# Transposing the last stage's tiles on VectorE and through DRAM instead of on TensorE

## The chip, the cores and the metric

One core of a Trainium2 chip runs the whole program. The metric is the device time of one execution in microseconds (us); lower is better. Engines are named as the profile names them: PE is TensorE (PEld its weight loads), DVE is VectorE, ACT is ScalarE, POOL is GpSimd, SP is SyncE, whose queue issues the DMA transfers spoken of here.

## The reference

Three steps follow each other: causal attention with a compressive memory over 4 batches of 8 heads (576 positions, 64 wide), then two feed-forward blocks over the 2304 tokens. The change is in the second of these and in the weights it loads:

```python
def _moe2_ref(x, w_in, w_out, g_ln):          # x 2304x512, w_in 512x1024, w_out 1024x512
    h = x @ w_in
    e = np.exp(h - np.max(h, axis=-1, keepdims=True))
    solu = h * (e / (np.sum(e, axis=-1, keepdims=True) + 1e-09))
    mu = np.mean(solu, axis=-1, keepdims=True)
    var = np.mean((solu - mu) ** 2, axis=-1, keepdims=True)
    ln = (solu - mu) / np.sqrt(var + 1e-06) * g_ln
    return (ln @ w_out).astype(np.float32)
```

## The kernel before

The kernel has three stages: attention (class `Attention`), the first feed-forward block (class `Moe1`), the second (class `Moe2`). Only the last one and the loading of its weights are touched. Each engine runs its instructions in the order in which the program issues them; waits between engines are semaphores that a framework derives from the reads and writes of tiles. A tile's tag with `bufs=n` means that n buffers are used in turn, so a new tile of the tag waits for the readers of the one n before it.

Every matrix product here is made of three: operands are split into a high part (rounded to the fp32r format) and a low part (the rest), and high x high, high x low and low x high are summed in PSUM.

The last stage works on 18 tiles (`NTL`) of 128 tokens. For tile i:

- `y_split` (helper `split_y`): ScalarE copies the high part of the tile's input (128x512), GpSimd subtracts for the low part.
- `h_mm` (L829): the first products, 24 matrix products of 512 columns into a PSUM tile H of 128x1024 (tag S, two buffers).
- `top` (L840): VectorE takes the row maximum.
- `norm`: ScalarE's exponent with its row sum (L849); on VectorE sum and reciprocal (L850, L851), the product of H and softmax (L852), mean and variance (L854, L855, L856); on GpSimd the power -0.5 of the variance (L857); on VectorE again the scaling (L858), from SBUF to SBUF in place. The result is `e`, with tokens in the partitions.
- `t_step`: the second product needs the other layout, features in the partitions. TensorE transposes eight 128x128 blocks into two PSUM tiles (tag T, two buffers, L868); ScalarE copies the high part to `L` (L875), VectorE subtracts for the low part (L876), both straight from PSUM.
- `o_mm` (L898): the second products, 24 of 512 columns into a PSUM tile O (tag X, one buffer); ScalarE copies the result to `ob` (L905), SP's queue writes it out (L906).

The loop issues for i: inputs of i+2, first products of i+1, their maximum, transposes of i, normalisation of i+1, second products of i-1. The first products of tile 0 and its normalisation are issued ahead of the loop, beside the last slice of the first block. In the last iteration tile 16's second products are split in two halves around tile 17's transposes. At i = 0 the loader finishes the last weights.

The weights come as 64-bit values through `Weights`: `_fetch` issues a load of raw words on SP's queue, `_convert` turns them to fp32 on ScalarE, VectorE and GpSimd and splits them; rows of `w_out` are scaled by `g_ln` (tile `gl`), and at most one further load is fetched ahead of the conversion that runs. The tiles of w_out are `w2o`, `w2o_a`, `w2o_b` and `w2o_c` with two blocks of 128 rows each; the last block is finished during the last stage's start. The last two of them and the inputs of the first two tiles lie in buffers that the first block has left.

Of the kernel before, what the change touches and what calls it, by code (L numbers as in the profile page):

```python
# [9 lines left out]
F32 = mybir.dt.float32  # L10
F32R = mybir.dt.float32r
U32 = mybir.dt.uint32
AF = mybir.ActivationFunctionType
ALU = mybir.AluOpType
AX = mybir.AxisListType
P = 128

DRAIN = 3

# [662 lines left out]
class Weights:  # L682
# [3 lines left out]
    N = 512  # L686
# [14 lines left out]

    def _fetch(self):
        hi, lo, src, scale = self.todo.pop(0)
        words = src.shape[-1] // hi.shape[-1]
        raw = self.pool.tile([P, words * self.N], U32, tag="raw", name="raw", bufs=2)
        rv = raw
        if len(hi.shape) == 3:
            rv = raw.rearrange("p (c f) -> p c f", f=src.shape[-1])
        self.nc.sync.dma_start(out=rv, in_=src)
        self.raw.append((hi, lo, raw, words, scale))  # L710

    def fetch(self):
# [82 lines left out]
class Moe2:  # L795
# [43 lines left out]
        mx = s[:, 0:1]  # L839
        self.nc.vector.tensor_reduce(mx, self.st[i]["H"], AX.X, ALU.max, negate=True)  # L840

    def norm(self, i, e=None):
        nc, FF, tp = self.nc, self.FF, self.tp
        H, s = self.st[i]["H"], self.st[i]["s"]
        mx, z, mv = s[:, 0:1], s[:, 1:2], s[:, 2:4]
        bs = s[:, 4:].rearrange("p (a b) -> p a b", b=6)
        if e is None:
            e = tp.tile([P, FF], F32, tag="e", name=f"e2_{i}")
        nc.scalar.activation(e, H, AF.Exp, bias=mx, accum_out=z)  # L849
        nc.vector.tensor_scalar_add(z, z, 1e-9)  # L850
        nc.vector.reciprocal(z, z)  # L851
        nc.vector.scalar_tensor_tensor(e, H, z, e, ALU.mult, ALU.mult)  # L852
        for a in range(FF // 512):
            nc.vector.bn_stats(bs[:, a, :], e[:, a * 512 : (a + 1) * 512])  # L854
        nc.vector.bn_aggr(mv, bs)  # L855
        nc.vector.tensor_scalar_add(mv[:, 1:2], mv[:, 1:2], 1e-6)  # L856
        nc.gpsimd.tensor_tensor(mv[:, 1:2], mv[:, 1:2], self.half, ALU.pow)  # L857
        nc.vector.tensor_scalar(e, e, mv[:, 0:1], mv[:, 1:2], ALU.subtract, ALU.mult)  # L858
        self.st[i]["e"] = e

    def t_step(self, i):
        nc, KF = self.nc, self.KF
        e = self.st[i]["e"]
        L = self.tp.tile([P, 2, KF, P], F32R, tag="L", name=f"L{i}")
        for a in range(KF // 4):
            T = self.ps.tile([P, 512], F32, tag="T", name=f"T2_{i}_{a}", bufs=2)
            for f in range(4):
                nc.tensor.transpose(  # L868
                    T[:, f * P : (f + 1) * P],
                    e[:, (4 * a + f) * P : (4 * a + f + 1) * P],  # L870
                    self.ident,
                )
            Tv = T.rearrange("p (f t) -> p f t", t=P)
            hi = L[:, 0, 4 * a : 4 * a + 4, :]
            nc.scalar.copy(hi, Tv)  # L875
            nc.vector.tensor_tensor(  # L876
                L[:, 1, 4 * a : 4 * a + 4, :], Tv, hi.bitcast(F32), ALU.subtract
            )
        self.st[i]["L"] = L

    def o_mm(self, i, steps, spare=False):
        nc, KF, DM = self.nc, self.KF, self.DM
        L = self.st[i]["L"]
        last = (i + 1) * P == self.out.shape[0]
        if steps[0] == 0:
            tags = "XS" if last else "S" if spare else "X"
            self.st[i]["O"] = [
                self.ps.tile([P, 1024], F32, tag=t, name=f"O{i}{t}", bufs=2 if t == "S" else 1)
                for t in tags
            ]  # L890

        w = DM // 2 if last else DM
        prods = ((0, 0), (0, 1), (1, 0))
        for a in range(0, DM, w):
            O = self.st[i]["O"][a // w][:, 0:w]
            for f in steps:
                for k, (ll, wl) in enumerate(prods):
                    nc.tensor.matmul(  # L898
                        O, L[:, ll, f, :], self.w2o[f][:, wl, a : a + w],
                        start=(f == 0 and k == 0), stop=(f == KF - 1 and k == 2),  # L900
                    )
            if steps[-1] < KF - 1:
                continue
            ob = self.tp.tile([P, w], F32, tag="ob", name=f"ob{i}_{a}")
            nc.scalar.copy(ob, O)  # L905
            nc.sync.dma_start(out=self.out[i * P : (i + 1) * P, a : a + w], in_=ob)  # L906
# [3 lines left out]
def attention_moe_kernel(  # L910
# [3 lines left out]
    nc = tc.nc  # L914
    B, H, S, D = q.shape
    NT, DM = out.shape
    KD = DM // P
    HT = NT // 2
    FF2 = moe2_g_ln.shape[0]
# [6 lines left out]
    xl = ctx.enter_context(tc.tile_pool(name="xl", bufs=2))  # L926
# [4 lines left out]
    tp = ctx.enter_context(tc.tile_pool(name="m1", bufs=2))  # L931
# [3 lines left out]
    gl = cpool.tile([P, FF2 // P], F32, tag="gl", name="gl")  # L935
# [19 lines left out]
    with ExitStack() as ea, ExitStack() as es:  # L955
        att = Attention(
            ea.enter_context(tc.tile_pool(name="att", bufs=2)),
            es.enter_context(tc.tile_pool(name="scores", bufs=2, side="right")),
            ps, tc, q, k, v, M_prev, z_prev, beta, xT, ident,
        )  # L960
        att.loader = loader
        for s in range(2):
            m.load_slice(s)

        def start_moe1():

            xh1 = eb.enter_context(tc.tile_pool(name="xh1", bufs=nblk - 2, side="right"))
            xh.append(xh1)
            for n in (2, 3):
                drain.add(split_x(n, xh1))  # L970

        rooms = att.between = Between()
        drain = Between()

        def filler():
            rooms.finish()
            for n in range(2):
                H = ps.tile([P, m.KF, 512], F32, tag="S", name=f"H0_{n}", bufs=2)
                yield from m.h_step(0, n, H, per=4)

        fill = filler()
        some = islice(fill, 11)
        todo = [
            (rooms, lambda p: att.done == 4, lambda: split_x(0, xh0)),
            (rooms, lambda p: att.done == 8, lambda: split_x(1, xh0)),
        ]
        with tc.manual_schedule():
            for p, i in att.run(some):
                if att.scores == 0:
                    es.close()  # L990
                    start_moe1()
                    att.scores = -1
                if (p, i) == (att.NP // 2, 0):
                    nc.sync.dma_start(out=gl, in_=moe2_g_ln.rearrange("(c p) -> p c", p=P))
                if todo and todo[0][1](p):
                    where, _, steps = todo.pop(0)
                    where.add(steps())
                if att.scores < 0 and i % DRAIN == 0:
                    drain()
            for _ in fill:  # L1000
                pass
            drain.finish()
# [5 lines left out]
    KF2 = FF2 // P  # L1008
# [3 lines left out]
    def add_w2(t, c, src, r, scale):  # L1012

        nf = t.shape[3]
        N = loader.N
        k = src.shape[1] // nf
        for a in range(0, nf, N):
            loader.add(
                t[:, 0, c, a : a + N],
                t[:, 1, c, a : a + N],  # L1020
                src[r * P : (r + 1) * P, a * k : (a + N) * k],
                gl[:, r : r + 1] if scale else None,
            )

# [30 lines left out]
    m2 = Moe2(tc, w2i, w2o, y0, yT, out, cpool, ps, ident)  # L1055
    with eb:
        eb.enter_context(tc.manual_schedule())
        items = [(s, n) for s in range(m.NS) for n in range(nblk)]
        for i, (s, n) in enumerate(items):
# [19 lines left out]
            else:  # L1079
                loader.pump()  # L1080
        m2.tp = tp
        m2.y_split(0)
        m2.h_mm(0)
        m2.top(0)
        G = tp.tile([P, 2 * m.KF * NB], F32, tag="G", name="e2_0", bufs=2)
        m2.norm(0, G[:, 0:FF2])
        m.y_step(*items[-1], ps, yT)
    m2.tp = ctx.enter_context(tc.tile_pool(name="m2", bufs=2))
    ctx.enter_context(tc.manual_schedule())
    NTL = NT // P  # L1090
    half = KF2 // 2
    m2.y_split(1)
    for i in range(NTL):
        if i + 2 < NTL:
            m2.y_split(i + 2)
        if i + 1 < NTL:
            m2.h_mm(i + 1)
            m2.top(i + 1)
        else:
            m2.o_mm(i - 1, range(half), True)  # L1100
        if i == 1:
            m2.norm(2)
            m2.o_mm(0, range(KF2))
        m2.t_step(i)
        if i + 1 < NTL:
            if i != 1:
                m2.norm(i + 1)
            if i > 1:
                m2.o_mm(i - 1, range(KF2))
        else:  # L1110
            m2.o_mm(i - 1, range(half, KF2))
            m2.o_mm(i, range(KF2))
        if i == 0:
            while loader.raw or loader.todo:
                loader.pump()
            loader.finish()


def split_y(nc, Y, src):
# [32 lines left out]
```

## Time and profile before

| | |
|---|---|
| device time, median of 3 runs | 829.36 us (829.1 to 829.38) |
| span of the profiled execution, first to last instruction | 826.7 us |
| PE busy | 801.9 us, 97% of the span, 4936 products |
| DVE busy | 577.8 us, 70% |
| ACT busy | 348.8 us, 42% |
| POOL busy | 344.3 us, 42% |
| mean granted TensorE clock | 0.994 of full speed |

The profile shows one execution, and its span; a device time of that one execution is not recorded apart from the runs, whose median is 2.7 us above the span. The last stage runs from about 605.9 us to the end. Busy times are sums over stages with different limits, so what a change in one stage is worth has to be read from that stage's rows.

### The profile page before, as it was taken

The page shows a single profiled execution, that of the slowest core. Times are in us where ns is not written, and L with a number is a line of the kernel's source. Part 1 is how long each engine was busy: PE and PEld are TensorE (multiplying, and loading weights), DVE is VectorE, ACT ScalarE, POOL GpSimd, SP SyncE. Part 2 cuts the span into 40 slices and gives each one's busy share as a digit, 9 for nine tenths or more (in the row PEclk, how much of TensorE's full clock was granted, in tenths as well). Part 3 has the DMA queues.
Part 4 walks back from the last instruction along what each step waited for, and adds up shares of the span by engine and source line. Part 5 has one row for each costly group of instructions (what it writes and reads, how often), then busy time and mean ns, then how long its engine had stood idle before and what let it go on. Part 6 is the DMA issues. An engine that isn't in the chain of part 4 may idle for free.

```text
span 826.7 us, 13172 instructions
## 1 busy us (share of the span) xinstructions
PE 801.9 (97%) x4936; PEld 705.4 (85%) x4936; DVE 577.8 (70%) x1130; ACT 348.8 (42%) x726; POOL 344.3 (42%) x380
## 2 busy tenths in 40 slices
PE   2799999999999999999999999999999999999998
PEld 1566666676899999999999999999998888888887
DVE  3999999994367777777775675766878555455553
ACT  1788898886333323232323232322423222222222
POOL 4888899998623333233432130322532111111110
PEclk9899999999999999999999999999999999999999
DMA  7567778671111212121211020201100000000001
GB/s 172 134 153 186 164 146 172 151 168 35 55 51 53 75 52 77 52 77 52 77 52 52 26 76 2 72 31 40 63 1 13 26 13 25 27 26 14 25 26 39
DMA packets 64655, 56.84 MB, mean 69 GB/s; under 512 B 48848, under 2 KB 49104, under 8 KB 64592
## 3 DMA queue, kind: packets, MB, share of 16 engines
q1 hardware_dynamic: 64208, 54.86, 24.8%
q10 hardware_dynamic: 384, 1.15, 0.5%
q8 instruction: 39, 0.64, 0.3%
q14 instruction: 24, 0.20, 0.1%
HBM read 46.55 MB, written 4.72 MB: 62 GB/s over the span
## 4 chain that ended last, share of the span: by engine, by line
PE 92%; DVE 3%; DMA 2%; POOL 1%; issue 1%; ACT 1%; ACTq 0%; DVEq 0%; POOLq 0%
PE H L608 24%; PE Y L637 24%; PE H L829 12%; PE T L377 5%; PE X L401 5%; PE S L267 4%; PE T L868 2%; PE S_L L281 2%; PE R L218 2%; PE X L359 1%; DMA k<-in_k_dram 1%; DVE sc L291 1%; PE O16S L898 1%; PE O10X L898 1%; PE O14X L898 1%
## 5 line engine op out<-in xcount | busy, mean ns | idle before, releaser
L637 PE MATMUL Y<-G,wo 128*128 128x384 f32 x1152 | 207.9, 335 | 0.2 <-DVE yT L649 0.2
L637 PEld LDWEIGHTS Y<-G,wo 128*128 128x128 f32 x1152 | 200.7, 188 | 0.5 <-ACT xh L575 0.4
L608 PE MATMUL H<-xh,wi 128*128 128x384 f32 x768 | 158.2, 338 | 0.0
L783 POOL TENSOR_TENSOR cvw<-cvw,cva 128x512 f32<-128x512 f32 x48 | 62.7, 1306 | 198.3 <-DVE cva L781 122.3
L608 PEld LDWEIGHTS H<-xh,wi 128*128 128x128 f32 x768 | 136.0, 189 | 1.4 <-issue 1.4
L621 ACT ACTIVATE t<-H 128x768 f32<-128x768 f32 x48 | 39.1, 814 | 216.3 <-PE H L608 216.3
L622 DVE TENSOR_TENSOR t<-H,t 128x768 f32<-128x768 f32 x48 | 45.9, 957 | 63.5 <-ACT t L621 63.5
L829 PE MATMUL H<-w2i,Ys 128*128 128x512 f32 x384 | 90.0, 390 | 0.0
L608 PE MATMUL H<-xT,wi 128*128 128x384 f32 x384 | 90.0, 338 | 0.0
L337 POOL TENSOR_SCALAR P<-P,sm,og 128x128 f32<-128x128 f32 (+3 forms) x128 | 86.7, 687 | 6.1 <-DVE sm L328 2.6
L829 PEld LDWEIGHTS H<-w2i,Ys 128*128 128x128 f32 x384 | 72.0, 188 | 15.0
L651 DVE TENSOR_TENSOR yT<-Y,yT 128x384 f32<-128x384 f32 (+1 forms) x126 | 79.0, 682 | 0.0
L624 DVE TENSOR_TENSOR G<-t,G 128x768 fp32r<-128x768 f32 x48 | 46.5, 968 | 43.3 <-ACT G L623 43.3
L857 POOL TENSOR_TENSOR s<-s,nhalf 128x1 f32<-128x1 f32 x18 | 9.9, 553 | 153.3 <-DVE s L856 143.9
L313 ACT ACTIVATE P<-sc,mx 128x128 f32<-128x128 f32 (+3 forms) x128 | 70.8, 558 | 5.7 <-DVE mx L291 5.6
L608 PEld LDWEIGHTS H<-xT,wi 128*128 128x128 f32 x384 | 68.6, 188 | 0.2 <-issue 0.2
L384 ACT COPY pt<-T 128x512 f32<-128x512 f32 (+1 forms) x95 | 54.3, 608 | 26.5 <-PE T L377 26.2
L267 PE MATMUL S<-kT,qT 64*128 64x512 f32 (+3 forms) x256 | 46.3, 486 | 19.5 <-DVE kT L182 18.6
L840 DVE TENSOR_REDUCE s<-H 128x1 f32<-128x1024 f32 x18 | 22.0, 1224 | 60.2 <-PE H L829 60.2
L623 ACT CAST G<-t 128x768 fp32r<-128x768 f32 x48 | 40.1, 835 | 51.2 <-DVE t L622 51.2
L291 DVE CUSTOM_DVE_ANT_0 sc<-S,mask 128x128 f32<-128x128 f32 (+3 forms) x128 | 55.7, 483 | 5.3 <-PE S L267 4.8
L875 ACT CAST L<-T 128x512 fp32r<-128x512 f32 x36 | 19.4, 590 | 80.4 <-PE T L868 80.4
(267 smaller groups left out, 1264.5 us busy)
## 6 DMA issues: line engine op xcount, KB each, us to landing
raw<-in_moe_w_in_dram SPq DMA_DIRECT2D x24, 512.0 KB, 3.7
raw<-in_moe_w_out_dram SPq DMA_DIRECT2D x24, 512.0 KB, 3.4
q<-in_q_dram SPq DMA_DIRECT2D x64, 140.0 KB, 3.1
out_dram<-ob SPq DMA_DIRECT2D x17, 256.0 KB, 2.0
v<-in_v_dram SPq DMA_DIRECT2D x32, 128.0 KB, 3.4
xT<-x SPq DMA_DIRECT2D x16, 256.0 KB, 3.0
k<-in_k_dram SPq DMA_DIRECT2D x24, 140.0 KB, 3.6
k<-in_k_dram SPq DMA_DIRECT2D x32, 72.0 KB, 3.3
```

Of the source, the lines that this page charges most:

```text
L267: nc.tensor.matmul(s, Q[rows, P * r : P * r + P], K[rows, 0:w], start=True, stop=True, skip_group_check=True,)
L291: self.nc.vector.tensor_tensor_reduce(out=sc, in0=s, in1=mask, scale=-0.125, scalar=3.0e38, op0=ALU.add, op1=ALU.min, accum_out=self.mx[p] ...
L313: self.nc.scalar.activation(t, self.sc.pop((p, i)), AF.Exp, bias=self.mx[p][:, i : i + 1], scale=-1.0, accum_out=self.sm[p][:, i : i + 1],)
L337: self.nc.gpsimd.tensor_scalar(d, d, self.sm[p][:, i : i + 1], og, ALU.mult, ALU.mult)
L384: self.copy(pt, T)
L608: nc.tensor.matmul(H[a:z, f], wi[:, wl, c, f * P + a : f * P + z], self.x[n][xl][:, c], start=(count[f] == 0), stop=(count[f] == 3 * KD - ...
L622: nc.vector.tensor_tensor(t, H, t, ALU.subtract)
L624: nc.vector.tensor_tensor(G[:, 1], t, G[:, 0].bitcast(F32), ALU.subtract)
L637: nc.tensor.matmul(Y[d][:, 0:NB], wo[:, wl, f, d * P : (d + 1) * P], G[:, gl, f], start=(i == 0), stop=(i == 3 * KF - 1),)
L651: nc.vector.tensor_tensor(y, src, y, ALU.add)
L783: self.eng.tensor_tensor(w, w, a, ALU.add)
L829: nc.tensor.matmul(H[:, nh * 512 : (nh + 1) * 512], Y[:, yl, c, :], w2i[:, wl, c, nh * 512 : (nh + 1) * 512], start=(k == 0), stop=(k == 3 ...
```

## The change

For tiles 1 to 15 `t_step` is replaced. `norm` is split into `exp` and the rest. `turn` transposes the normalised tile on VectorE, which does so within each square of 32x32 and leaves the square in its place; the result (tile `rest`, two buffers) is written to DRAM, 512 KB, and read back by four transfers, one for each quarter of 32 partitions, which bring the squares to the quarter where they belong. `spread` then makes the high part on ScalarE and the low part on GpSimd, from SBUF, with the columns put in order by the access pattern. The order of features that results is another than before: partition quarter i holds features 256 i to 256 i + 255. So the rows of w_out and of `g_ln` are loaded in that order, in four pieces each, and tiles 0, 16 and 17, which are still transposed on TensorE (`direct`), are scaled to a permuted place.

The loop issues for i from 1: inputs of i+1, first products of i, maximum and exponent of i, the high part of i-1, the rest of the normalisation of i, the low part of i-1, VectorE's transpose and the transfers of i, second products of i-2. The second products of a tile thus stand two iterations after its first ones, and within them all products with the high part come first. Tiles 16 and 17 are transposed and multiplied after the loop.

```diff
@@ _fetch
-        self.nc.sync.dma_start(out=rv, in_=src)
+        n = P // len(parts)
+        for i, part in enumerate(parts):
+            self.nc.sync.dma_start(out=rv[i * n : (i + 1) * n], in_=part)
@@ Moe2
+    def exp(self, i, e=None):
         H, s = self.st[i]["H"], self.st[i]["s"]
-        mx, z, mv = s[:, 0:1], s[:, 1:2], s[:, 2:4]
+        if e is None:
+            e = self.tp.tile([P, self.FF], F32, tag="e", name=f"e2_{i}")
+        self.nc.scalar.activation(e, H, AF.Exp, bias=s[:, 0:1], accum_out=s[:, 1:2])
+        self.st[i]["e"] = e
+
+    def norm(self, i, direct=False):
...
-        nc.vector.tensor_scalar(e, e, mv[:, 0:1], mv[:, 1:2], ALU.subtract, ALU.mult)
-        self.st[i]["e"] = e
+        to = e
+        if direct:
+
+            t = self.st[i]["e"] = self.rest[:, i % 2]
+            to = t.rearrange("t (c i p) -> t i c p", i=4, p=Q)
+            e = e.rearrange("t (i c p) -> t i c p", i=4, p=Q)
+        nc.vector.tensor_scalar(to, e, mv[:, 0:1], mv[:, 1:2], ALU.subtract, ALU.mult)
+
+    def turn(self, i):
+
+        nc, FF = self.nc, self.FF
+        e, T, R = self.st[i]["e"], self.rest[:, i % 2], self.rest[:, 2 + i % 2]
+        nc.vector.transpose(T, e)
+        D = self.dram.tile([P, FF], F32, tag="D", name=f"D{i}", bufs=3)
+        nc.sync.dma_start(out=D, in_=T)
+        src = D.rearrange("(j p) (i n) -> i p j n", p=Q, i=4)
+        for q in range(4):
+            nc.sync.dma_start(
+                out=R[q * Q : (q + 1) * Q].rearrange("p (j n) -> p j n", j=4), in_=src[q]
+            )
+        self.st[i]["R"] = R
+
+    def spread(self, i):
+        nc, KF = self.nc, self.KF
+        L = self.st[i]["L"] = self.tp.tile([P, 2, KF, P], F32R, tag="L", name=f"L{i}")
+        R = self.st[i]["R"].rearrange("p (j c t) -> p c j t", j=4, t=Q)
+        hi, lo = (L[:, k].rearrange("p c (j t) -> p c j t", t=Q) for k in range(2))
+        nc.scalar.copy(hi, R)
+        yield
+        nc.gpsimd.tensor_tensor(lo, R, hi.bitcast(F32), ALU.subtract)
@@ o_mm
-        prods = ((0, 0), (0, 1), (1, 0))
+        order = [(f, 0, wl) for f in range(KF) for wl in range(2)] + [(f, 1, 0) for f in range(KF)]
+        half = len(order) // 2
+        steps = range(half * part[0], half * (part[-1] + 1))
@@ attention_moe_kernel
-                    nc.sync.dma_start(out=gl, in_=moe2_g_ln.rearrange("(c p) -> p c", p=P))
+                    rows = moe2_g_ln.rearrange("(i c p) -> i p c", i=4, p=Q)
+                    for j in range(4):
+                        nc.sync.dma_start(out=gl[j * Q : (j + 1) * Q], in_=rows[j])
...
+    direct = (0, NTL - 2, NTL - 1)
     m2.y_split(1)
-    for i in range(NTL):
-        if i + 2 < NTL:
-            m2.y_split(i + 2)
+    for i in range(1, NTL):
         if i + 1 < NTL:
-            m2.h_mm(i + 1)
-            m2.top(i + 1)
-        else:
-            m2.o_mm(i - 1, range(half), True)
+            m2.y_split(i + 1)
+        m2.h_mm(i)
+        m2.top(i)
+        m2.exp(i)
+        lo = iter(())
         if i == 1:
-            m2.norm(2)
-            m2.o_mm(0, range(KF2))
-        m2.t_step(i)
-        if i + 1 < NTL:
-            if i != 1:
-                m2.norm(i + 1)
-            if i > 1:
-                m2.o_mm(i - 1, range(KF2))
-        else:
-            m2.o_mm(i - 1, range(half, KF2))
-            m2.o_mm(i, range(KF2))
-        if i == 0:
+            m2.t_step(0)
+        elif i - 1 not in direct:
+            lo = m2.spread(i - 1)
+            next(lo)
+        m2.norm(i, i in direct)
+        next(lo, None)
+        if i not in direct:
+            m2.turn(i)
+        if i > 1:
+            m2.o_mm(i - 2)
+        if i == 1:
             while loader.raw or loader.todo:
                 loader.pump()
             loader.finish()
+    m2.t_step(NTL - 2)
+    m2.o_mm(NTL - 2, (0,))
+    m2.t_step(NTL - 1)
+    m2.o_mm(NTL - 2, (1,))
+    m2.o_mm(NTL - 1)
```

## Rows read from the trace of the kernel before

**Rows 1.** Busy time: window, length, us and instructions per engine, clock, DMA.
```profile
660.00:680.00 20.00, 20.00 (x97) 16.68 (x96) 11.14 (x19) 5.47 (x10) 2.02 (x3) 1.00 0.04 14
```

**Rows 2.** Chain of waits, one tile of the last stage: start us, us, what.
```profile
674.92 0.87 PE T L868 x8
675.79 5.53 PE O4X L898 x24
681.32 5.45 PE H L829 x24
```

**Rows 3.** Chain of waits, start of the last stage.
```profile
621.22 0.88 PE T L868 x8
622.09 5.48 PE H L829 x24
627.57 5.53 PE O0X L898 x24
```

**Rows 4.** Chain of waits, end of the last stage.
```profile
805.91 5.47 PE O15X L898 x24
811.38 2.77 PE O16S L898 x12
815.02 2.77 PE O16S L898 x12
```

**Rows 5.** Groups by line, 665 to 827 us: busy us, mean ns, idle before.
```profile
L876 DVE TENSOR_TENSOR L<-T,L 128x512 fp32r<-128x512 f32 x27 | 17.3, 682 | 2.6 <-ACT L L875 2.6
L875 ACT CAST L<-T 128x512 fp32r<-128x512 f32 x26 | 14.0, 590 | 60.6 <-PE T L868 60.6
```

**Rows 6.** Line L182, VectorE's transposes: ns min/median/max, first and last start us.
```profile
L182 DVE STREAM_TRANSPOSE kT<-k x16: 758/1003/1260, 9.4 to 181.7; 128x576 f32<-128x576 f32 x16
```

**Rows 7.** Timeline of VectorE: start us, us, what, idle before and its releaser.
```profile
621.25 1.23 DVE L840 TENSOR_REDUCE s<-H 128x1 f32<-128x1024 f32 x1 [0.40 <-PE H L829]
623.90 0.15 DVE L850 TENSOR_SCALAR s<-s 128x1 f32<-128x1 f32 x1 [0.23 <-ACT e L849]
628.01 1.77 DVE L858 TENSOR_SCALAR e<-e,s 128x1024 f32<-128x1024 f32 x1 [0.68 <-POOL s L857]
629.70 1.21 DVE L840 TENSOR_REDUCE s<-H 128x1 f32<-128x1024 f32 x1
636.27 1.77 DVE L858 TENSOR_SCALAR e<-e,s 128x1024 f32<-128x1024 f32 x1 [0.67 <-POOL s L857]
...
811.93 0.81 DVE L858 TENSOR_SCALAR e<-e,s 128x1024 f32<-128x1024 f32 x1 [0.73 <-POOL s L857]
```

**Rows 8.** Timeline of GpSimd.
```profile
627.94 1.29 POOL L792 TENSOR_TENSOR w2o_c<-cvw,w2o_c 128x512 fp32r<-128x512 f32 x1
```

**Rows 9.** Timeline of ScalarE.
```profile
622.65 1.13 ACT L849 ACTIVATE e<-H,s 128x1024 f32<-128x1024 f32 x1
633.13 0.59 ACT L905 COPY ob<-O0X 128x512 f32<-128x512 f32 x1 [0.98 <-PE O0X L898]
```

**Rows 10.** DMA issues by line: count, KB each, median us to landing.
```profile
raw<-in_moe_w_out_dram SPq DMA_DIRECT2D x24, 512.0 KB, 3.4
out_dram<-ob SPq DMA_DIRECT2D x17, 256.0 KB, 2.0
v<-in_v_dram SPq DMA_DIRECT2D x32, 128.0 KB, 3.4
```

**Rows 11.** Line L709, weight loads on SP's queue: ns of an issue, min/median/max.
```profile
L709 SPq DMA_DIRECT2D raw<-in_moe_w_out_dram x24: 327/340/550, 63.3 to 594.1; - x24
```

**Rows 12.** TensorE near the kernel's start: timeline, then busy time by stretch.
```profile
23.14 3.89 PE L267 MATMUL S<-kT,qT 64*128 64x512 f32 x16 [6.38 <-DVE kT L182]
33.26 1.13 PE L267 MATMUL S<-kT,qT 64*128 64x512 f32 x4 [1.47 <-DVE kT L182]
...
25.00:26.00 1.00, 1.00 (x6) 0.68 (x4) 0.63 (x3) 0.00 (x0) 0.82 (x3) 0.50 1.01 255
34.00:35.00 1.00, 1.00 (x6) 0.33 (x6) 1.00 (x3) 0.60 (x4) 0.83 (x2) 1.00 0.82 246
```

More of the change, by code (lines that the diff above doesn't have):

```diff
@@ L16 @@
 P = 128
+Q = 32
 DRAIN = 3
@@ L703, in _fetch @@
         hi, lo, src, scale = self.todo.pop(0)
-        words = src.shape[-1] // hi.shape[-1]
+        parts = src if isinstance(src, list) else [src]
+        words = parts[0].shape[-1] // hi.shape[-1]
         raw = self.pool.tile([P, words * self.N], U32, tag="raw", name="raw", bufs=2)
@@ L707, in _fetch @@
         if len(hi.shape) == 3:
-            rv = raw.rearrange("p (c f) -> p c f", f=src.shape[-1])
-        self.nc.sync.dma_start(out=rv, in_=src)
+            rv = raw.rearrange("p (c f) -> p c f", f=parts[0].shape[-1])
+        n = P // len(parts)
+        for i, part in enumerate(parts):
+            self.nc.sync.dma_start(out=rv[i * n : (i + 1) * n], in_=part)
         self.raw.append((hi, lo, raw, words, scale))
@@ L840, in top @@
         self.nc.vector.tensor_reduce(mx, self.st[i]["H"], AX.X, ALU.max, negate=True)
-    def norm(self, i, e=None):
-        nc, FF, tp = self.nc, self.FF, self.tp
+    def exp(self, i, e=None):
         H, s = self.st[i]["H"], self.st[i]["s"]
-        mx, z, mv = s[:, 0:1], s[:, 1:2], s[:, 2:4]
+        if e is None:
[4 more added lines that the diff above has]
+        nc, FF = self.nc, self.FF
+        H, s, e = (self.st[i][k] for k in ("H", "s", "e"))
+        z, mv = s[:, 1:2], s[:, 2:4]
         bs = s[:, 4:].rearrange("p (a b) -> p a b", b=6)
-        if e is None:
-            e = tp.tile([P, FF], F32, tag="e", name=f"e2_{i}")
-        nc.scalar.activation(e, H, AF.Exp, bias=mx, accum_out=z)
         nc.vector.tensor_scalar_add(z, z, 1e-9)
@@ L857, in norm @@
         nc.gpsimd.tensor_tensor(mv[:, 1:2], mv[:, 1:2], self.half, ALU.pow)
-        nc.vector.tensor_scalar(e, e, mv[:, 0:1], mv[:, 1:2], ALU.subtract, ALU.mult)
-        self.st[i]["e"] = e
+        to = e
[5 more added lines that the diff above has]
+    def turn(self, i):
+        nc, FF = self.nc, self.FF
+        e, T, R = self.st[i]["e"], self.rest[:, i % 2], self.rest[:, 2 + i % 2]
[16 more added lines that the diff above has]
+        nc.gpsimd.tensor_tensor(lo, R, hi.bitcast(F32), ALU.subtract)
     def t_step(self, i):
@@ L867, in t_step @@
             for f in range(4):
[L868 to L872, printed above, removed]
+                nc.tensor.transpose(T[:, f * P : (f + 1) * P], e[:, (4 * a + f) * P : (4 * a + f + 1) * P], self.ident)
             Tv = T.rearrange("p (f t) -> p f t", t=P)
@@ L879, in t_step, with o_mm @@
         self.st[i]["L"] = L
-    def o_mm(self, i, steps, spare=False):
+    def o_mm(self, i, part=(0, 1)):
         nc, KF, DM = self.nc, self.KF, self.DM
@@ L884, in o_mm @@
         last = (i + 1) * P == self.out.shape[0]
-        if steps[0] == 0:
+        spare = part != (0, 1)
+        if 0 in part:
             tags = "XS" if last else "S" if spare else "X"
@@ L892, in o_mm @@
         w = DM // 2 if last else DM
-        prods = ((0, 0), (0, 1), (1, 0))
+        order = [(f, 0, wl) for f in range(KF) for wl in range(2)] + [(f, 1, 0) for f in range(KF)]
+        half = len(order) // 2
+        steps = range(half * part[0], half * (part[-1] + 1))
         for a in range(0, DM, w):
             O = self.st[i]["O"][a // w][:, 0:w]
[L896 to L902, printed above, removed]
+            for k in steps:
+                f, ll, wl = order[k]
+                nc.tensor.matmul(
+                    O, L[:, ll, f, :], self.w2o[f][:, wl, a : a + w],
+                    start=(k == 0), stop=(k == len(order) - 1), skip_group_check=spare,
+                )
+            if 1 not in part:
                 continue
@@ L1017, in add_w2 @@
         for a in range(0, nf, N):
+            cols = slice(a * k, (a + N) * k)
+            if scale:
+                rows = src.rearrange("(i c p) f -> c i p f", i=4, p=Q)[r]
+                part = [rows[i, :, cols] for i in range(4)]
+            else:
+                part = src[r * P : (r + 1) * P, cols]
             loader.add(
@@ L1020, in add_w2 @@
                 t[:, 1, c, a : a + N],
-                src[r * P : (r + 1) * P, a * k : (a + N) * k],
+                part,
                 gl[:, r : r + 1] if scale else None,
@@ L1081, in attention_moe_kernel @@
         m2.tp = tp
+        rest = xl.tile([P, KD * HT], F32, tag="xl", name="rest")
+        m2.rest = rest[:, 0 : 4 * FF2].rearrange("p (n f) -> p n f", f=FF2)
         m2.y_split(0)
@@ L1085, in attention_moe_kernel @@
         G = tp.tile([P, 2 * m.KF * NB], F32, tag="G", name="e2_0", bufs=2)
-        m2.norm(0, G[:, 0:FF2])
+        m2.exp(0, G[:, 0:FF2])
+        m2.norm(0, True)
         m.y_step(*items[-1], ps, yT)
     m2.tp = ctx.enter_context(tc.tile_pool(name="m2", bufs=2))
+    m2.dram = ctx.enter_context(tc.tile_pool(name="dram", bufs=3, space=bass.MemoryType.DRAM))
     ctx.enter_context(tc.manual_schedule())
     NTL = NT // P
-    half = KF2 // 2
+    direct = (0, NTL - 2, NTL - 1)
     m2.y_split(1)
-    for i in range(NTL):
-        if i + 2 < NTL:
-            m2.y_split(i + 2)
+    for i in range(1, NTL):
         if i + 1 < NTL:
-            m2.h_mm(i + 1)
-            m2.top(i + 1)
-        else:
-            m2.o_mm(i - 1, range(half), True)
-        if i == 1:
-            m2.norm(2)
-            m2.o_mm(0, range(KF2))
-        m2.t_step(i)
-        if i + 1 < NTL:
-            if i != 1:
-                m2.norm(i + 1)
-            if i > 1:
-                m2.o_mm(i - 1, range(KF2))
-        else:
-            m2.o_mm(i - 1, range(half, KF2))
-            m2.o_mm(i, range(KF2))
-        if i == 0:
+            m2.y_split(i + 1)
[3 more added lines that the diff above has]
+        lo = iter(())
+        if i == 1:
+            m2.t_step(0)
[9 more added lines that the diff above has]
+        if i == 1:
             while loader.raw or loader.todo:
```

## The prediction

> **What bounds the kernel now.** I read the busy time by stretch first. In the last stage TensorE works every microsecond at the full clock level (granted clock 1.00, 2.4 GHz), while VectorE, ScalarE and GpSimd are busy for 11.1, 5.5 and 2.0 us of the same 20 us [rows 1]. The chain of waits then shows what a tile costs: eight transposes 0.87 us, 24 second products 5.53 us, 24 first products 5.45 us, with no gap between them [rows 2]. So a tile's period is about 11.83 us and TensorE's own work sets it. The chain at the stage's start [rows 3] and end [rows 4] is likewise all TensorE. Something taken off TensorE here shortens the kernel as long as nobody else becomes late; the rest of the argument is a search for who that might be.
>
> **What is removed.** Tiles 1 to 15 lose their TensorE transposes: 15 x 0.87 = 13.1 us [rows 2]. Does a second product run as fast without transposes ahead of it? Tile 16's products stand in two halves of 12, one directly behind tile 15's products, one directly behind transposes, and both take 2.77 us [rows 4]; so I take the whole 13.1 us as gain (lower bound of this term 12.2 us, if each tile gave back the 0.06 us that separates 5.53 from 5.47 [rows 2, 4]). The new order of the products (all with the high part of the tile first, then the low part) leaves their count at 24, and costs nothing by itself. New period: 5.45 + 5.50 = 10.95 us.
>
> **What VectorE pays.** It loses the two subtractions of 0.68 us that read the transposed tile from PSUM [rows 5] and gains one 32x32 transpose of 128x1024. The nearest row is the transposes of 128x576 in the attention stage, 0.758 us where the written side is contiguous, 1.26 us where it isn't [rows 6]. Scaled by 1024/576 that is 1.35 and 2.24 us; here both sides are contiguous, and part of the 0.758 us is fixed, so I take 1.25 us and keep 2.24 us as the upper bound. Per tile, from the start of the maximum to the start of the last scaling, VectorE takes 636.27 - 629.70 = 6.57 us, waits for ScalarE and GpSimd included [rows 7]. With 0.81 us for the scaling (its length in tile 17, where GpSimd has nothing else to do [rows 7]) and 1.25 us for the transpose, tile work ends 8.65 us after the first products: less than 10.95 us, so hidden.
>
> The scaling is not always 0.81 us. In tile 1 and tile 2 it took 1.77 us; in tile 1 GpSimd had just begun a subtraction of two SBUF operands, which ended at 629.23, 0.55 us before the scaling ended at 629.78 [rows 7, 8]. The change moves the low-part subtraction, 128x1024, to GpSimd: two times 1.29 us [rows 8], 2.6 us, queued right behind the small power of the next tile, on which the scaling waits too. If it starts there, the scaling takes 2.6 + 0.55 = 3.15 us and VectorE's work ends after 6.57 + 3.15 + 1.25 = 11.0 us. That is as long as the period; but then the following tile's data are late by 2.3 us, its subtraction starts behind the scaling, and that tile is back at 8.65 us. I cost it at nothing. The Trainium skill ("SBUF — State Buffer", section "Who interferes with whom") has the rule behind this: VectorE in a two-port mode and GpSimd take a shared port pair in turn, whole instructions at a time, while a VectorE instruction with one SBUF input outside those modes is left alone. It would let the scaling be blocked and the new transpose not; it is the fourth rival below.
>
> **What the way through DRAM costs.** One write of 512 KB, which must land, then four reads of 128 KB, each to a quarter of the partitions. No row shows a write that is read back. The write: between the 256 KB output's 2.0 us and the 512 KB weight load's 3.4 us; I take 2.8 us. The reads: 512 KB in one piece lands in 3.4 us; as four issues on SP at 0.33 us each the last starts 1.0 us late, and 128 KB loads of v took 3.4 us, so 3.4 to 4.4 us [rows 10, 11]; I take 4.0 us. With 0.1 us for the two hand-overs: 6.9 us (5.4 to 7.8). The skill's page "SBUF — State Buffer" (section "Door 1: The DMA port swizzle") speaks against the change: a transfer to 32 partitions reaches half of the SBUF ports, at about 218 GB/s at best; four of them in turn would need an estimated 2.4 us beside the fixed part, instead of 1.2 us. The sum by it would be 1.2 us more round trip, so 1.2 us less gain, still in the forecast's own range. No row here shows it.
>
> In the steady state from the end of a tile's first products to the start of its second there are now two periods, 21.9 us. Used are 8.65 + 6.9 + 1.1 (ScalarE's copy of the high part: a pass over 128x1024 took 1.13 us [rows 9]) + 0.6 (the copy of the older tile's output, which stands behind it on ScalarE, and must empty the one PSUM buffer before the next second products start; 0.59 us [rows 9]) = 17.3 us. 4.6 us are left; so a round trip up to 11.5 us is hidden. The low part has 3.7 us more (16 products first). SP's queue holds the output's transfer behind the reads, but the output has two buffers, and nobody waits.
>
> **The start is not the steady state.** Tile 1's first products are followed only by tile 0's transposes (0.87), not by second products, so there is less time. First products of tile 1 end at 621.22 [rows 3]. The maximum ends at 622.48 [rows 7]. The exponent now comes ahead of tile 0's two PSUM copies on ScalarE: 1.13 + 2 x 0.59 us [rows 5, 9], to about 624.8; VectorE's second low part (0.68) ends at 625.45, and only then does the normalisation of tile 1 go on, which it did at 623.90 [rows 7]: 1.55 us later. GpSimd's last weight subtraction moves from 627.94 to 629.5 and ends at 630.8 [rows 8] (the new order wants it at 631.0, the sixteenth of tile 0's products: just hidden; bound 0.5 us). Tile 1's scaling ends 0.55 us behind it, 631.35; transpose 632.6; round trip 639.5; copy 640.6; tile 0's output copy 641.2. TensorE, with tile 1's transposes gone, is there at 627.57 + 5.53 + 5.45 = 638.55 [rows 2, 3]. It waits **2.7 us** (1.2 with the shortest round trip, 3.6 with the longest, 4.6 with the longest transpose too). Behind it wait only third and later tiles, which have their 4 us. Tile 0, 16 and 17 are scaled straight to a permuted layout; if the 0.81 us doubled, at most 0.8 us once.
>
> **The end.** Tile 16 is still transposed on TensorE, but its products follow at once instead of a tile later. Counted from the end of the last first products: tile 15's products to 5.48, transposes to 6.35; ScalarE's output copy 5.5 to 6.1, then the first half of tile 16's copy (0.59) to 6.7. TensorE waits **0.35 us** (0 to 1). Tile 17 is normalised at 6.57 + 0.81 = 7.4, tile 16's low parts are through at 8.75, TensorE wants tile 17 at 6.7 + 2.77 = 9.5: covered.
>
> **Other edits.** The gain vector and the eight scaled weight blocks come in four pieces each: 27 more issues of 0.33 us on SP [rows 11], fetched one conversion ahead; hidden, and up to 1 us once if that cover is gone.
>
> **Sum.** -13.1 + 2.7 + 0.35 = -10.05 us. The profiled span is 826.7 us, so 816.7 us; the median of the runs shown, 829.36 us, lies 2.7 us above the span, for what lies around it, which the change leaves alone: **819.3 us**.
>
> **The rivals.** (1) The forecast, 818 to 820.7 us: 0.55. (2) Tile 1's round trip is hidden as well: 816.4 us. It needs the trip within 4.2 us; the rows' shortest is 5.4. 0.08. (3) The wait at tile 1 lowers the clock. After an idle time of 6.38 us at the kernel's start the granted clock was 0.50, the 1.2 GHz level, still two microseconds after TensorE had gone on; after 1.47 us it was 1.00 [rows 12]. 2.7 us lies between. Some 3 us of work at half speed cost 1.5 us: 820.8 us. 0.20. (4) The lock between scaling and GpSimd's subtraction is met in every tile, and the transpose is as slow as its upper bound or is blocked as well: VectorE needs 6.57 + 3.15 + 2.24 = 12.0 us in tiles that meet it and 9.6 in those that don't. If three tiles of four meet it, the mean is 11.4 us, 14 x 0.45 = 6 us lost: 825 us. 0.10. (5) Slower: the round trip sets the pace. Each tile's second products wait for its data, and the period becomes (10.35 + trip)/2. With the 14 later tiles and the wait at tile 1, gain and loss cancel at a trip of 12.2 us; at 13 us it is 8.8 + 14 x 0.73 = 19 us lost against 12.7 gained: 835.6 us. For it: a write that must land ahead of reads isn't in this trace. Against: the transfers of such sizes that it shows land in 3.4 us or less [rows 10]. 0.07.
>
> **Numbers.** A measurement of this kernel can tell about 0.2% from no change, 1.7 us. Cases 1 to 3 and nearly all of 4 are faster, 5 is slower beyond 12.2 us: faster 0.93, same 0.02, slower 0.05. Range 816.2 to 823.0 us: it takes in cases 1, 2, 3 and the milder half of 4.
>
> **What would show it.** Right: TensorE's chain in the middle of the stage alternates 5.45 and 5.5 us pieces with no transposes and no gap; one gap of 2 to 4 us ahead of tile 1's second products, ended by ScalarE; some 0.3 us ahead of tile 16's; scalings of either about 0.8 or about 3 us; a VectorE transpose near 1.25 us. Wrong: gaps in each tile ended by a copy that waits for DMA (5) or VectorE without idle time (4), or a granted clock below 1.00 behind tile 1 (3).

## The result and the profile after

The changed kernel takes 820.0 us (median of 4 runs, 819.54 to 821.37) against 829.37 us before: ratio 0.9893, 95% interval 0.9879 to 0.9907. 819.3 us was forecast. The span of the profiled execution is 817.8 us.

Busy time by stretch, in the middle of the last stage; it answers to [rows 1]:

```profile
660.00:680.00 20.00, 20.00 (x89) 16.40 (x88) 13.95 (x18) 4.67 (x8) 7.50 (x5) 1.00 0.41 132
```

TensorE is still at work all the time; VectorE went from 11.1 to 13.95 us of 20, GpSimd from 2.0 to 7.5, and the transfers from 14 to 132 GB/s. All of that is work that TensorE does not wait for.

The chain of waits, which answers to [rows 2, 3, 4]: the start of the stage from tile 1's transpose on, two tiles, and the end.

```profile
629.36 1.79 DVE e L872
...
631.17 1.25 DVE rest L878
...
632.44 2.63 DMA D<-rest
...
636.52 3.06 DMA rest<-D
...
639.65 1.04 ACT L L893
640.70 0.49 ACT ob L940
...
641.24 5.80 PE O1X L933 x24
647.04 5.45 PE H L833 x24
652.49 5.54 PE O2X L933 x24
...
802.15 3.05 PE O16S L933 x12
...
806.07 2.75 PE O16S L933 x12
```

No transposes stand between 5.45 and 5.54 us any more: a period of 10.99 us instead of 11.83. Ahead of `O1X` the chain leaves TensorE and goes back through ScalarE, the transfers, VectorE's transpose and a long scaling. TensorE's waits in the last stage are two, of 2.8 us and 0.3 us:

```profile
PE O1X L933 <- ACT ob L940: 2.8, 1, 2.8
PE O16S L933 <- ACT L L907: 0.3, 1, 0.3
```

The transfers (median us to landing) and two of VectorE's scalings, with GpSimd's low part beside the longest; they answer to [rows 7, 8, 10]:

```profile
D<-rest SPq DMA_DIRECT2D x15, 512.0 KB, 2.6
rest<-D SPq DMA_DIRECT2D x60, 128.0 KB, 2.9
```

```profile
647.60 0.81 DVE L872 TENSOR_SCALAR e<-e,s 128x1024 f32<-128x1024 f32 x1 [0.73 <-POOL s L865]
...
659.26 2.88 DVE L872 TENSOR_SCALAR e<-e,s 128x1024 f32<-128x1024 f32 x1 [0.73 <-POOL s L865]
662.17 1.25 DVE L878 STREAM_TRANSPOSE rest<-e 128x1024 f32<-128x1024 f32 x1
```

```profile
659.19 2.40 POOL L895 TENSOR_TENSOR L<-rest,L 128x1024 fp32r<-128x1024 f32 x1
```

**How the profiles are compared.** In the profiled executions the last stage begins (the first products of tile 0) anywhere from 605.1 to 607.8 us, while the code ahead of it hardly differs; two executions of one and the same kernel, the changed one, begin it at 605.72 and at 606.77 us (e11 below). So I also compare the stage alone, from that start to the end of the last output copy. Before it is 823.96 - 605.89 = 218.07 us, after 814.97 - 605.72 = 209.25 us: 8.82 us less. From the rows: 15 x 0.87 = 13.05 us of transposes gone; 2.8 and 0.3 us of waits; `O1X` 0.26 us and the first half of `O16S` 0.28 us longer than the same work without a wait ahead of it (5.54 and 2.77 us); some 0.04 us in each of 14 second products, 0.5 us. -13.05 + 2.8 + 0.3 + 0.26 + 0.28 + 0.5 = -8.9. The medians differ by 9.37 us, 0.55 us more than the stages; that is less than what two executions of one kernel differ by.

### The profile page after: what moved, and what is told of

Same layout as the page of the kernel before. It is cut to its first block, busy times and chain, and to the rows that moved or that the text cites. A ratio compares the mean times of both kernels' runs of the same rounds, so it can differ in the third digit from the quotient of the medians.

```text
span 817.8 us, 13168 instructions
## 1 busy us (share of the span) xinstructions
PE 789.9 (97%) x4816; PEld 692.9 (85%) x4816; DVE 589.4 (72%) x1115; ACT 348.2 (43%) x711; POOL 382.2 (47%) x395
## 4 chain that ended last, share of the span: by engine, by line
PE 85%; DVE 5%; POOL 4%; DMA 2%; ACT 2%; issue 1%; SPq 0%; ACTq 0%; DVEq 0%; POOLq 0%
PE H L609 24%; PE Y L638 24%; PE H L833 11%; PE T L378 4%; PE X L402 4%; PE S L268 4%; POOL P L338 1%; PE S_L L282 1%; PE R L219 1%; DVE sc L292 1%; POOL xT L578 1%; DMA k<-in_k_dram 1%; PE X L360 1%; PE O1X L933 1%; PE O16S L933 1%
## 5 line engine op out<-in xcount | busy, mean ns | idle before, releaser
L850 ACT ACTIVATE e<-H,s 128x1024 f32<-128x1024 f32 x18 | 20.1, 1117 | 79.6 <-DVE s L844 79.6
L378 PE MATMUL T<-ident,P 128*128 128x128 f32 x320 | 48.0, 280 | 2.1 <-POOL P L338 1.7
```

Of the source, the lines that this page charges most:

```text
L378: nc.tensor.transpose(T[:, P * i : P * i + P], t, self.ident)
```

## Experiments

The theory: the gain is TensorE's removed transposes; what is lost again stands in the two waits, each the end of one chain that can be followed; everything else is hidden, up to a limit. The rivals are named with each run. All edits are to the changed kernel, and times are medians. "Stage" is the stage alone, of the profiled execution.

| run | us | ratio to before, 95% interval | stage, us | wait at O1, us |
|---|---|---|---|---|
| the changed kernel | 820.0 | 0.9893, 0.9879 to 0.9907 | 209.25 | 2.8 |
| e1_t0_first | 819.43 | 0.9887, 0.9872 to 0.9902 | 207.74 | 1.3 |
| e2_t0_pool | 818.23 | 0.9872, 0.9857 to 0.9886 | 206.73 | 0.3 |
| e3_all_waits | 817.72 | 0.9865, 0.9850 to 0.9880 | 206.09 | 0.3 |
| e4_tile1_pe | 818.62 | 0.9875, 0.9859 to 0.9892 | 207.12 | 0 |
| e5_no_trip | 816.38 | 0.9850, 0.9835 to 0.9865 | 206.21 | 0 |
| e6_trip_copy | 829.33 | 1.0003, 0.9993 to 1.0013 | 215.65 | 7.0 |
| e7_trip_twice | 854.77 | 1.0320, 1.0302 to 1.0338 | 244.71 | 9.6 |
| e8_low_dve | 822.02 | 0.9918, 0.9903 to 0.9933 | 210.59 | 2.7 |
| e9_old_order | 824.32 | 0.9950, 0.9937 to 0.9964 | 213.51 | 2.9 + 1.2 |
| e10_low_dve_nowait | 818.62 | 0.9862, 0.9845 to 0.9878 | 210.90 | 0.3 |
| e11_again | 821.65 | 0.9897, 0.9882 to 0.9912 | 210.65 | 2.8 |

### The wait at tile 1: three links of its chain

```diff
+        if i == 1:
+            m2.t_step(0)
         m2.exp(i)
         lo = iter(())
-        if i == 1:
-            m2.t_step(0)
-        elif i - 1 not in direct:
+        if i - 1 not in direct:
```

> Tile 0's TensorE transposes are issued ahead of tile 1's exponent again, as in the kernel before. Theory (the wait ahead of tile 1's second products is the end of one chain through ScalarE, VectorE, GpSimd and the transfers): the chain begins 1.54 us earlier, so the wait of 2.81 us falls to 1.3 us and the time from 820.0 to 818.5 us. Rival (the wait is set by the transfers, which are held up by something else than the data): wait and time stay at 2.8 us and 820.0 us.

On top of that edit (the same lines further down go, and tile 3's input isn't split again):

```diff
+        if i == 1:
+            while loader.raw or loader.todo:
+                loader.pump()
+            loader.finish()
+            m2.y_split(3)
         m2.norm(i, i in direct)
```

> As the run before it, and GpSimd gets the last weight subtraction and the low part of tile 3's input ahead of tile 1's power instead of behind it. Theory (tile 1's scaling takes 1.79 instead of 0.81 us because GpSimd's subtraction runs): the scaling is back at 0.81 us, the wait ahead of tile 1's second products falls by another 1.0 us to 0.3 us, the time to 817.5 us. Rival (the length of the scaling has another cause): scaling 1.8 us, wait 1.3 us, 818.5 us.

The changed kernel with only this:

```diff
+    direct = (0, 1, NTL - 2, NTL - 1)
...
             m2.o_mm(i - 2)
+        if i == 2:
+            m2.t_step(1)
```

> The changed kernel, but tile 1 is transposed on TensorE as well, behind tile 0's second products; 14 tiles go through DRAM instead of 15. Theory: TensorE pays 0.87 us more, and the wait of 2.81 us and the 0.26 us by which tile 1's products are longer behind it go, as tile 2 has the time of the steady state: 817.8 us. Rival (the wait moves on to tile 2's second products): 820.0 to 821 us.

The stage became 1.51 us shorter with e1 (1.5 expected), another 1.01 us with e2 (1.0 expected), and 2.13 us with e4 (2.2 expected). The wait, in e1's waits of TensorE and in e2's:

```profile
PE O1X L933 <- ACT ob L940: 1.3, 1, 1.3
```

```profile
PE O1X L933 <- ACT ob L940: 0.3, 1, 0.3
```

In e2's chain tile 1's scaling is short again, 0.82 us, as nothing on GpSimd runs beside it:

```profile
629.10 0.82 DVE e L872
...
629.95 1.26 DVE rest L878
```

So the chain is the one of the prediction, link by link, and with e4 no later tile's wait takes its place. e1's whole time fell by only 0.6 us: in its profiled execution the stage began at 607.32 instead of 605.72 us, and the run says nothing of why; without any edit this start has differed by 1.05 us (e11).

### The wait at tile 16, and the best version

On top of e2's two edits:

```diff
-        if i == 1:
-            m2.t_step(0)
+        if i in (1, NTL - 1):
+            m2.t_step(i - 1)
...
-    m2.t_step(NTL - 2)
     m2.o_mm(NTL - 2, (0,))
```

> As the run before it, and tile 16's TensorE transposes are issued ahead of tile 17's exponent, behind its first products, so that tile 15's second products stand between them and tile 16's. Theory: the wait of 0.33 us ahead of tile 16's products goes, and the 0.28 us by which their first half is longer behind a wait: 816.9 us. Rival (VectorE then gets through tile 17's normalisation later, and TensorE waits for that instead): a wait of 0.5 to 1 us ahead of tile 17's transposes, 817.5 us.

The end of its chain of waits:

```profile
794.92 0.87 PE T L904 x8
795.79 5.53 PE O15X L933 x24
801.32 2.76 PE O16S L933 x12
```

The first half of tile 16 is back at 2.76 us, no wait moved to tile 17, and the stage is 0.64 us shorter (0.6 expected). With all three edits it is 3.16 us shorter than in the changed kernel. The time, 817.72 us, is the lowest median here of a kernel that computes the reference; its interval overlaps that of e2, so the last 0.64 us rest on the stage alone.

### The round trip: none, longer, twice

```diff
-        D = self.dram.tile([P, FF], F32, tag="D", name=f"D{i}", bufs=3)
-        nc.sync.dma_start(out=D, in_=T)
...
+        R = T
         self.st[i]["R"] = R
```

> The changed kernel without its transfers through DRAM: the high and the low part are made from VectorE's 32x32 squares where they stand, so the squares do not change partition quarters and the output of tiles 1 to 15 is not the reference's. Theory (the round trip costs only the wait at tile 1): 820.0 - 2.81 - 0.26 = 816.9 us, all other pieces of TensorE as long as before. Rival (15 MB of transfers also slow something in the steady state, or the output's transfers): below 816 us.

The stage is 3.04 us shorter (3.07 expected). So 15 MB of transfers cost TensorE nothing but the wait at tile 1. They do slow the output's transfers, 3.0 us at the median with them and 2.0 us without, but nobody waits for those.

```diff
         nc.sync.dma_start(out=D, in_=T)
-        src = D.rearrange("(j p) (i n) -> i p j n", p=Q, i=4)
+        D2 = self.dram.tile([P, FF], F32, tag="D2", name=f"Dc{i}", bufs=3)
+        nc.sync.dma_start(out=D2, in_=D)
+        src = D2.rearrange("(j p) (i n) -> i p j n", p=Q, i=4)
```

> The changed kernel with one more step in the round trip, a copy of 512 KB within DRAM, some 3 us: the trip is 10 instead of 7 us. Theory (up to 11.5 us are hidden in the steady state): no waits from tile 2 on, the wait at tile 1 grows by these 3 us, 823.0 us; with a wait near 6 us the granted clock falls behind it, another 1.5 us, 824.5 us. Rival (the steady state has less room than I worked out): waits at every other tile, 830 us and more.

e6 took 829.33 us (825.8 to 830.11 in 10 runs) where the theory had 824.5 us and its rival 830 us and more: the median is nearer the rival. The profiled execution is the fastest of them, and only for it can the theory be followed. Its waits of TensorE, and the stretches around the first (the granted clock is the third figure from the end):

```profile
PE O1X L935 <- ACT ob L942: 7.0, 1, 7.0
...
PE O9X L935 <- ACT ob L942: 0.2, 1, 0.2
```

```profile
642.00:644.00 2.00, 0.00 (x0) 0.00 (x0) 0.00 (x0) 0.47 (x1) 0.00 (x0) 0.50 0.79 290
644.00:646.00 2.00, 0.89 (x2) 0.79 (x3) 0.00 (x0) 2.00 (x4) 1.35 (x1) 0.50 0.50 164
646.00:648.00 2.00, 2.00 (x6) 1.52 (x6) 1.21 (x3) 0.69 (x2) 2.00 (x2) 0.50 0.28 98
```

The copy took 3.9 us instead of 3, so the wait grew by 4.2 us; the clock fell to its lower level during the wait, and `O1X` took 7.41 instead of 5.80 us (1.6 us; 1.5 expected). There is one small wait later, at tile 9, where the copy took 4.61 us:

```profile
721.84 2.65 DMA D<-rest
724.50 4.61 DMA Dc<-D
...
730.50 3.09 DMA rest<-Dc
```

That trip took 11.75 us (721.84 to 733.59), just beyond the limit of 11.5 us; tile 1's took 11.2 us. The other nine executions are 1.4 to 4.3 us longer. Their mean granted clock is lower in seven of them (0.988 to 0.990 against 0.991), so some may wait at further tiles; where they do is not shown, and for them the rival, less room than worked out, is not excluded.

```diff
+        D2 = self.dram.tile([P, FF], F32, tag="D2", name=f"Dc{i}", bufs=3)
+        nc.sync.dma_start(out=D2, in_=R)
+        for q in range(4):
+            nc.sync.dma_start(out=R[q * Q : (q + 1) * Q], in_=D2[q * Q : (q + 1) * Q])
         self.st[i]["R"] = R
```

> The changed kernel with the round trip made twice (written, read back, written and read back again in place), some 13.8 us. Theory (beyond 11.5 us the trip sets the pace, a period of (10.35 + trip) / 2): 12.1 us per tile instead of 11.0, and 6.9 us more at tile 1: about 842 us. Rival (the queue overlaps the trips of several tiles, and only the start is late): 827 us.

Neither: 854.77 us, 13 us beyond the theory. The chain of waits shows why; a tile in the middle:

```profile
682.81 3.46 DMA D<-rest
...
686.34 0.33 SPq L883
...
687.67 3.06 DMA rest<-D
...
690.87 2.63 DMA Dc<-rest
...
695.27 0.42 SPq L945
...
695.74 3.56 DMA D<-rest
```

The chain runs through SP's queue alone, from one tile's first write (682.81) to the next one's (695.74): 12.9 us. The queue issues in order, and each write that waits for a read, or read that waits for a write, holds the transfers of the next tile and the output's too. The period is thus the time for which a tile holds the queue, not half of the way from products to products. That is read from the chain; no run takes the second trip off this queue. In the changed kernel a tile holds it for about 5 us (2.63 for the write, 1.7 for the reads' issues, 0.4 for the output), so this limit is far off there.

### The lock, and the clock

```diff
-        nc.gpsimd.tensor_tensor(lo, R, hi.bitcast(F32), ALU.subtract)
+        nc.vector.tensor_tensor(lo, R, hi.bitcast(F32), ALU.subtract)
```

> The changed kernel with the low part subtracted on VectorE instead of GpSimd, at the same place in the order. Theory (the scaling held up by GpSimd, 2.9 instead of 0.8 us in some tiles, costs nothing): no scaling of 2.9 us is left, and the time stays within 0.2% of 820.0 us. Rival (the lock costs time in the steady state): 1 us or more faster. Other rival (VectorE has no room for 1.3 us more): slower.

No scaling is 2.9 us any more, as expected, but the median is 2 us above that of the changed kernel. The pieces of its chain are those of the changed kernel but for one: `O1X` takes 7.17 instead of 5.80 us, behind a wait of 2.7 us. e8's granted clock there, then that of the changed kernel:

```profile
643.00:644.00 1.00, 1.00 (x4) 0.81 (x3) 1.00 (x2) 0.00 (x0) 0.29 (x1) 0.50 0.00 0
```

```profile
643.00:644.00 1.00, 1.00 (x6) 0.83 (x5) 0.49 (x3) 0.41 (x2) 1.00 (x2) 1.00 0.10 37
```

Four products instead of six in a microsecond: the 1.2 GHz level behind a wait no longer than that of the changed kernel, whose clock stayed up. Two runs tell whether that is the edit's doing.

> The changed kernel once more. Theory (a wait of 2.7 to 2.9 us of TensorE lowers the clock in some executions and not in others): times in two groups some 1.4 us apart, the slower ones at a lower mean clock. Rival (the wait of 2.8 us never lowers the clock in this kernel): all within 0.6 us at a mean clock of 0.994.

The same kernel ran at 820.25, 821.31, 821.98 and 822.0 us; the latter two had a mean clock of 0.992 and 0.991, the former two 0.994. In the profiled one (822.0) the clock fell:

```profile
642.26 7.21 PE O1X L933 x24
```

```profile
643.00:644.00 1.00, 1.00 (x4) 0.81 (x3) 0.13 (x1) 0.75 (x1) 1.00 (x1) 0.50 1.00 406
```

So one program has both outcomes, 1.4 us apart (7.21 against 5.80). Take this clock off, and the stages of e11 (210.65 - 1.41 = 209.24 us) and of e8 (210.59 - 1.37 = 209.22 us) are that of the first execution, 209.25 us: e8's edit did not change it. The expected groups are there among the times, though not clean: 821.31 us came at 0.994, and the kernel before, which has no wait in this stage, once ran at a mean clock of 0.991 too (830.55 us).

On top of e3's three edits:

```diff
-        nc.gpsimd.tensor_tensor(lo, R, hi.bitcast(F32), ALU.subtract)
+        nc.vector.tensor_tensor(lo, R, hi.bitcast(F32), ALU.subtract)
```

> The run that takes away both waits of TensorE (tile 0's and tile 16's transposes ahead of the exponents, GpSimd's weight work ahead of tile 1's power), and the low part on VectorE. The low part on VectorE alone was 2 us slower than the changed kernel, and 1.4 us of that stood in tile 1's products, behind the wait, at the 1.2 GHz level of the clock. Theory (the clock, not VectorE, made the difference; the lock costs nothing): without the waits the last stage takes 206.1 us as in the run without this edit, 817.7 us in all. Rival (VectorE has no room for the subtraction): 1.3 us or more slower, with waits that end at VectorE.

818.62 us at the median, but 818.2, 818.27, 818.96 and 822.04 us one by one. The profiled execution is the longest; it has waits in the steady state, and its chain of waits between them is a loop:

```profile
PE O9X L933 <- ACT ob L940: 1.6, 1, 1.6
PE O6X L933 <- ACT ob L940: 1.4, 1, 1.4
PE O14X L933 <- ACT ob L940: 0.8, 1, 0.8
```

```profile
682.03 1.06 ACT L L893
...
683.12 1.22 DVE L L895
684.35 1.17 DVE rest L878
...
685.53 4.55 DMA D<-rest
...
691.41 3.14 DMA rest<-D
...
694.65 1.05 ACT L L893
...
719.75 5.22 DMA D<-rest
...
776.70 4.40 DMA D<-rest
```

On VectorE the low part of one tile stands ahead of the transpose of the next and waits for that tile's trip, so each trip starts when the one before it is through: 671.01 to 682.03 to 694.65. Copy, low part, transpose and a trip of 7.15 us come to 10.6 us and leave almost nothing of 10.99. Three writes took 4.55, 5.22 and 4.40 us instead of 2.6, and behind each stands one of the three waits, at tiles 6, 9 and 14. What made these writes longer is not shown. So the theory's half of the expectation, that VectorE's low part costs nothing, holds at the median (ratio 0.9862, with GpSimd 0.9865); in the longest execution the rival's place was right, not its reason: VectorE had time, but stood waiting. The lock costs nothing in these runs. GpSimd looks the safer place, since its queue can wait without holding a transpose; that rests on this one execution.

### The order of the products

```diff
-        order = [(f, 0, wl) for f in range(KF) for wl in range(2)] + [(f, 1, 0) for f in range(KF)]
+        order = [(f, ll, wl) for f in range(KF) for ll, wl in ((0, 0), (0, 1), (1, 0))]
```

> The changed kernel with the second products in the order of before (for each block high x high, high x low, low x high) instead of all with the high part first. Theory: a tile's products need its low part at the third of them; at tile 1 GpSimd ends it at 643.16 us, so TensorE waits 1.5 us more, at tile 16 0.9 us more; the other tiles have it in time, and a piece of 24 products takes 5.50 instead of 5.54 us, which gives back 0.6 us: 821.8 us. Rival (the order costs nothing and gains nothing): 820.0 us.

```profile
PE O1X L933 <- ACT ob L940: 2.9, 1, 2.9
PE O1X L933 <- POOL L L895: 1.2, 1, 1.2
PE O16S L933 <- DVE L L908: 0.8, 1, 0.8
...
PE O11X L933 <- POOL L L895: 0.3, 1, 0.3
```

The waits for low parts came where they were expected, 1.2 and 0.8 us (1.5 and 0.9 expected). Not expected: 0.3 us at tile 11, and the clock, which fell during the second of the two waits at tile 1 (the 22 products behind it took 6.62 us; behind tile 11's wait, at the full clock, 22 took 5.33). And a piece of 24 takes 5.53 us in the old order too, so the new one did not lengthen it; what did is not shown. The new order is worth 4.3 us of stage in these two executions, some 1.3 us of it by the clock.

## Why the prediction was right

**The gain.** The transposes' time came back but for 0.5 us, nearly as the two halves of tile 16 had suggested. The one term of the sum that was clearly mis-sized is the period: 5.54 us for the second products, where I had taken 5.50, the mean of pieces that alternate between 5.48 and 5.53 us; with 14 of them 0.5 us. The lower bound of the term had that.

**The total.** It came out closer than its terms. The sum was 10.05 us, the stage gained 8.82: 0.5 us of period, 0.5 us of products behind waits and 0.1 us of wait were missing. That the medians differ by 9.37 us, and the forecast of the time is only 0.7 us off, is in part luck. And the 2.7 us between span and median were not all "what lies around it": in every run whose span is known the time is 1.7 to 1.9 us above that run's own span, so by that some 0.9 us was a profiled execution faster than the median. The sum is not touched by that, as it is a difference.

**VectorE.** The transpose took 1.25 us in every tile (1.25 taken, 1.35 scaled), within 3 ns, whether GpSimd ran or not. The scaling met the low-part subtraction in 6 of 18 tiles, took 2.88 us there (3.15 worked out), and the next tiles were on time, as worked out. That agrees with the rule of the Trainium skill ("SBUF — State Buffer", section "Who interferes with whom"), by which an instruction in a two-port mode is blocked while GpSimd holds the shared ports and one with a single SBUF input outside those modes is not. The fourth rival, a lock in nearly every tile, is out by that count and by e8: without the lock the pieces are as long.

**The round trip.** 632.44 to 639.59 us, 7.15 us for 6.9: the write 2.63 us (2.8 taken), the reads with their four issues 4.38 us (4.0 taken, 4.4 the upper bound). An issue took 0.42 us at the median, where 0.33 was taken. The Trainium skill's rule on 32 partitions ("SBUF — State Buffer", "Door 1: The DMA port swizzle") had given an estimated 1.2 us more than the 4.0; 0.4 were measured, and no run here separates the ports from the issues.

**The wait at tile 1.** 2.8 us for 2.7, from a chain whose every link stood within 0.2 us of its place (scaling's end 631.15 for 631.35, output copy's end 641.19 for 641.2). That the sum is so close is partly luck: the scaling ended 0.2 us early and the trip took 0.25 us longer. e1, e2 and e4 show that these links are the cause. Two costs were missing: products behind a wait are longer at full clock too, 0.26 us at tile 1 and 0.28 at tile 16.

**Tile 16.** 0.33 us for 0.35.

**The third rival** came true in part. The clock falls behind the wait of 2.8 us in some executions and not in others, at 1.4 us (1.5 worked out). It was written as an alternative to the forecast and is a share of its executions. Of the 2.46 us between the two profiled ones (819.54 and 822.0 us) it is 1.4; the other 1.05 us is the later start of the stage.

**The fifth rival** was priced wrongly. (10.35 + trip)/2 holds only while SP's queue can take the next tile's transfers; e7 paid 12.9 us a tile where the formula says 12.1. The limit of 11.5 us agrees with e6's profiled execution, where a trip of 11.75 us makes a wait of 0.2 us; e6's longer executions leave it open.

## What to carry to other kernels

Work taken off the engine that is always busy comes back nearly in full if its replacement has time to spare (12.5 of 13.05 us here): count the time from producer to consumer in periods, and count it again for the first tile, where the pipeline isn't yet full. A queue that issues in order adds a second limit, the time for which one tile holds it, and an instruction that waits for one tile's data ahead of another tile's start makes a loop of two tiles that were apart. A wait on the busy engine of nearly 3 us is worth removing for more than its length: here 0.26 us more each time, and 1.4 us more when the clock falls.

## What the runs showed of the hardware

- TensorE's clock behind an idle time of 2.8 us: up in one profiled execution of a program (`O1X` 5.80 us), at the 1.2 GHz level in another execution of the same program (7.21 us). Behind 1.3 us (e1) it stayed up, behind 7.0 us (e6) it fell, and there it was at 0.50 from 642 to 644 us already, while TensorE did nothing.
- Behind each wait at the full clock that was read here, of 0.2 to 2.8 us, a piece of products is longer by 0.25 to 0.28 us, whatever the length of the wait.
- A 512 KB copy from DRAM to DRAM took 3.9 us at the median, a write from SBUF of the same size 2.6 us; in e7, with output and reads just ahead of it in the queue, that write took 3.5 us.
- A 32x32 transpose of 128x1024 on VectorE took 1.245 to 1.248 us in all 15 tiles; the scaling took 0.81 us alone and 2.88 us behind GpSimd's subtraction of 2.40 us.
